# Strassen's seven products for a block's first matrix product, with the weight sums streamed from DRAM

## The chip, the cores and the metric

The kernel runs on one core of one Trainium2 chip, as one launch. The metric is the device time of the launch in microseconds (us), lower is better. A change of 0.5% (4.9 us) is about what a measurement of this kernel can tell from no change.

## The reference: what is computed

Causal attention with a decay, and then two feed-forward blocks, each a product up (512 to 2048), an elementwise function, and a product down (2048 to 512). The chain runs over 2304 tokens in float32:

```python
attn = softmax(q @ k.T / 8 + decay, causal); x = attn @ v      # 4 batches x 8 heads, 576 x 64 each
h = x @ w_in1                                                   # 2304x512 @ 512x2048
g = where(h >= 1, h, where(h <= -1, 0, (h + 1) ** 2 / 4))
x = g @ w_out1                                                  # 2304x2048 @ 2048x512
h = x @ w_in2                                                   # the product that is changed
P = a[0] + a[1] * h + a[2] * h**2 + a[3] * h**3
g = P / (1 + abs(b[0]) * abs(h) + abs(b[1]) * h**2 + 1e-6)
out = g @ w_out2
```

The weights come as 64-bit floats and are turned into 32-bit ones on the chip.

## The kernel before

Matmuls run on float32 operands of reduced width ("fp32r"). To keep the accuracy, each operand is split into a high part (a cast) and a low part (the rest), and each product is three matmuls: low by high, high by low, high by high. So for every tile ACT makes the high part and DVE or POOL the low one.

**Stages.** Attention (with early pieces of the first block as filler) takes the first 200 us or so. Then the first block runs to about 595 us and the second from there to the end. The tokens are cut into four chunks of 512 and one of 256 (`CH`, L698), the 2048 hidden columns into 16 groups `g` of 128. The second block takes one chunk after the other; for each of the 16 groups it does

- `gemm_in` (L728): 4 pieces of the contraction by 3 matmuls, each 128x128 weights by 128x512 tokens, into one PSUM bank `h`;
- `b_abs`, `b_sq`, `b_lin` (ACT, L769 to L776), `b_v` (POOL, L780), `b_t1`, `b_t2` (DVE, L784, L788), `b_ln`, `b_exp` (ACT, L791, L794), `b_t3`, `b_v3`, `b_t4` (DVE, L798, L801, L805): the rational function. After `b_t4` the bank `h` is free;
- `split_g_hi` (ACT, L745) and `split_g_lo` (POOL, L749);
- `gemm_out` (L820): four token pieces by 3 matmuls into four accumulators `a0` to `a3`, which stand in PSUM over all 16 groups.

There are four `h` banks (`HB`) and four accumulators: all eight banks of PSUM. At the end of a chunk the accumulators are copied out (`out_copy`) and stored.

**Weights.** Each 128x512 piece is loaded (`w_raw`), put together by one ACT and four DVE instructions (`w_steps`, L86), and, for those not needed yet, stored to DRAM (`w_store`) and loaded again later (`w_load`), cast and subtracted (`w_split`). That work for the second block lies in the first block's time, 42 such stores and loads in all. In the second block all its weights stand in SBUF.

**Order.** The program is written as tasks with a key, an engine or a choice of engines, an estimated duration, and the buffers that it takes and frees. `plan` (L273) places them one by one by the earliest start plus a small weight on the key, and the instructions are then written out in that order. Each engine runs its own list strictly in that order; what was estimated only decides the order. Loads and stores are all issued by SP, in order.

Of the kernel before, what the change touches and what calls it, by code (L numbers as in the profile page):

```python
# [7 lines left out]
F32 = mybir.dt.float32  # L8
# [10 lines left out]
def kernel(ctx, tc, qT, kT, v, f, w_in1, w_out1, w_in2, w_out2, a, b, out):  # L19
# [9 lines left out]
    P = 128  # L29
# [49 lines left out]
    wfd = dram.tile([2, NF, 2, P, DM], F32, name="wfd")  # L79

# [5 lines left out]
    def w_steps(m, g, half):  # L86
# [33 lines left out]
    def w_split(m, g, half):  # L120
        at = {}

        def s0():
            pool = wearly if g < W_EARLY else wpool["late"]
            at["s"] = wst.pop((m, g, half))
            at["w"] = [pool.tile([P, DM], F32R, tag=f"{x}{half}_{g}", name=f"w{x}{half}_{m}_{g}") for x in "hl"]
            ACT.copy(at["w"][0][:], at["s"])

        def s1(eng=POOL):
            hi, lo = at["w"]  # L130
            eng.tensor_tensor(out=lo[:], in0=at["s"], in1=hi[:].bitcast(F32), op=ALU.subtract)
# [116 lines left out]
    XR = 4  # L248
    XA = 3
# [3 lines left out]
    N_BUF = dict(S=SB, T=TB_, O=OB, P=PB, PT0=1, PT1=1, q=2, k=2, qs=2, ks=2, v=2, R=RB, x=1, cb=2, g=W_EARLY, c=2, s=SF, xa=XA, xr=XR, po=2, raw=2, d=2)  # L253
# [489 lines left out]
    def split_g_hi(g, n):  # L743
        gt[g] = [gp.tile([P, NM], F32R, tag=y, name=y)[:, 0:n] for y in ("gh", "gl")]
        ACT.copy(gt[g][0], mid[g][0])  # L745
# [74 lines left out]
    def gemm_out(m, x, g, d, first, last):  # L820
# [5 lines left out]
        for y, (gg, ww) in enumerate(((gl, wh), (gh, wl), (gh, wh))):  # L826
# [3 lines left out]
            else:  # L830
                PE.matmul(acc[x, d], gg[:, dd], ww[:], start=st, stop=sp)  # L831
# [17 lines left out]
    def out_copy(x, d, eng):  # L849
        os_[x, d] = stage.tile([P, DM], F32, tag="raw", name="osb", bufs=2)  # L850
        copy(eng, os_[x, d][:], acc.pop((x, d)))

    def out_store(x, d):
        t0 = C0[x % NCH] + d * P
        SP.dma_start(out[t0:t0 + P, :], os_.pop((x, d))[:])

# [89 lines left out]
    TN = 5, 5, 5  # L946
# [3 lines left out]
    CK, CL, W2S, W2L = 0.4, 10.0, 20.0, 3.0  # L950
# [3 lines left out]
    KXL = 1.0  # L954
    LOE = ['pool']
# [19 lines left out]
    passes = [(0, x, early) for x in range(FILL, HEAD)] + [(0, x, late) for x in range(HEAD)]  # L975
    passes += [(0, x, range(NF)) for x in range(HEAD, NCH)]
    passes += [(1, x, range(NF)) for x in range(NCH, 2 * NCH)]
# [14 lines left out]
    bufs.update({tag: [t_end] * k for tag, k in dict(h=HB, g=GB, t0=TN[0], t1=TN[1], t2=TN[2], raw=2, d=2, xr=XR, a0=1, a1=1, a2=1, a3=1).items()})  # L992
    bufs.update({f"x{k}": [] for k in range(KD)})


# [17 lines left out]
    prev_in = None  # L1013
    for p, (m, x, fs) in enumerate(passes):
# [3 lines left out]
        ca, cs, cd, cp = cost("act", n), cost("act", n, "ps"), cost("dve", n), cost("pool", n)  # L1018

        sx = [] if p else sx0  # L1020
        for kk in range(KD) if p else ():
            deps = [evac[x - NCH, kk]] if m == 1 else xstores(x, kk)
            t = xload = task(k0 - KXL, "sp", ld(n), lambda x=x, kk=kk: x_load(x, kk), deps + [xload], ("xr",))
            t = task(k0 - 0.5, "act", ca, lambda x=x, kk=kk: split_x_hi(x, kk), [t] + sx[:1], (f"x{kk}",))
            sx.append(task(k0 - 0.5, "dve", cd, lambda x=x, kk=kk: split_x_lo(x, kk), (t,), (), ("xr",)))
# [3 lines left out]
        if add:  # L1029
            for d in range(KD):  # L1030
                loads[d] = task(
                    k0 + 1, "sp", ld(n), lambda x=x, d=d: part_load(x, d), [lastpass[x, d]] + list(prev_evac), ("t2",)
                )
        outs = []
        for g in fs:
            key = base + sizes[p, g]
            one, end = g == fs[0], g == fs[-1]

            for kks in [(kk,) for kk in range(KD)] if one or end else [range(KD)]:
                deps = [prev_in, wd[m, g, 0]] + [sx[kk] for kk in kks if one]  # L1040
                prev_in = task(key, "pe", mm(n, 3 * len(kks)), lambda m=m, x=x, g=g, kks=kks: gemm_in(m, x, g, kks), deps,
                               ("h",) if kks[0] == 0 else (), tuple(f"x{kk}" for kk in kks) if end else ())
            t = tin = prev_in
# [17 lines left out]
            t = task(key, "act", ca, lambda g=g, n=n: split_g_hi(g, n), (t,), ("g",))  # L1061
            t = task(key, "pool", cp, lambda g=g: split_g_lo(g, POOL), (t,), (), ("t1",))

            for d in range(nd):
# [79 lines left out]
```

## Time and profile before

| | |
|---|---|
| median of 3 runs | 983.75 us (982.46 to 986.32) |
| profiled execution, first to last instruction | 984.3 us |
| PE (matmul) busy | 98% of the span |
| DVE, ACT, POOL busy | 74%, 64%, 46% |
| DMA | 125.15 MB, mean 127 GB/s |

The profiled execution has no time of its own beside its span; the span lies 0.55 us above the median of the runs. "Busy" is the time in which an engine had an instruction in it. Matmuls overlap: one of 128x512 is shown as some 0.39 us long, though the next starts 0.23 us later, so rates are read from starts. The profile names a group of instructions by line, engine and operation, with "output <- inputs".

### The profile page before, as it was taken

To read this page: it belongs to the slowest core of one execution; us is meant where nothing else is said; L and a number is where in the kernel's file an instruction comes from. 1 tells how busy PE (TensorE), PEld (TensorE's weight loads), DVE (VectorE), ACT (ScalarE), POOL (GpSimd) and SP (SyncE) were. 2 spreads that over 40 slices of the span, in tenths; PEclk is the share of its full clock that TensorE was granted. 3 is DMA by queue.
4 is the path that set the end of the run, shared out by engine and by line. 5 is a ranking of instruction groups with operands and counts; after the bars stand their busy time and mean duration, and the time that the engine had idled before them with its cause. 6 is when DMAs were issued, how large, how long until landed. Compare 5 with 4: busy or idle time off the path is not lost.

```text
span 984.3 us, 15503 instructions
## 1 busy us (share of the span) xinstructions
PE 964.6 (98%) x5124; PEld 784.3 (80%) x5124; DVE 729.0 (74%) x1379; ACT 629.6 (64%) x1324; POOL 457.0 (46%) x505
## 2 busy tenths in 40 slices
PE   8988999999999999999999999999999999999998
PEld 5656777777888788888888998888888888888887
DVE  7999888883876977877875679776667667666656
ACT  6988688884654433424333579776777667666666
POOL 4877746654655422222221225544444454444444
PEclk9999999999999999999999999999999999999999
DMA  6878589844563365665643651010101100010010
GB/s 224 260 258 251 174 272 293 263 162 166 194 232 118 96 226 155 188 205 161 221 151 123 177 172 33 1 44 1 43 1 44 43 1 22 0 43 1 1 44 22
DMA packets 66657, 125.15 MB, mean 127 GB/s; under 512 B 10048, under 2 KB 20944, under 8 KB 66576
## 3 DMA queue, kind: packets, MB, share of 16 engines
q1 hardware_dynamic: 66576, 124.16, 39.6%
q8 instruction: 40, 0.66, 0.3%
q14 instruction: 41, 0.34, 0.1%
HBM read 94.61 MB, written 29.51 MB: 126 GB/s over the span
## 4 chain that ended last, share of the span: by engine, by line
PE 85%; DVE 6%; DMA 3%; issue 2%; ACT 2%; SPq 1%; POOL 1%; DVEq 0%; POOLq 0%; ACTq 0%
PE h L735 38%; PE a L831 19%; PE a L829 17%; PE T L510 3%; PE O L547 2%; PE a L816 2%; PE S L446 2%; DVE P L486 1%; DVE xl L724 1%; DMA cb<-cd 1%; DMA R<-rcd 1%; PE S L437 1%; ACT P L498 1%; DVE wd L97 1%; DVE PT L360 0%
## 5 line engine op out<-in xcount | busy, mean ns | idle before, releaser
L749 POOL TENSOR_TENSOR gl<-t,gh 128x512 fp32r<-128x512 f32 (+1 forms) x160 | 195.4, 1222 | 292.1 <-ACT gh L745 224.8
L735 PE MATMUL h<-xl,wh 128*128 128x512 f32 (+1 forms) x640 | 236.7, 370 | 1.0 <-DVE xl L724 0.6
L735 PE MATMUL h<-xh,wl 128*128 128x512 f32 (+1 forms) x640 | 237.0, 370 | 0.0
L735 PE MATMUL h<-xh,wh 128*128 128x512 f32 (+1 forms) x640 | 235.7, 368 | 0.0
L745 ACT CAST gh<-t 128x512 fp32r<-128x512 f32 (+1 forms) x160 | 92.9, 581 | 124.0 <-PE a L831 47.9
L780 POOL TENSOR_TENSOR t<-t,t 128x512 f32<-128x512 f32 (+1 forms) x80 | 94.5, 1182 | 126.7 <-ACT t L773 121.1
L735 PEld LDWEIGHTS h<-xl,wh 128*128 128x128 f32 x640 | 120.8, 189 | 24.0 <-DVE xl L724 4.2
L735 PEld LDWEIGHTS h<-xh,wl 128*128 128x128 f32 x640 | 120.9, 189 | 20.4
L735 PEld LDWEIGHTS h<-xh,wh 128*128 128x128 f32 x640 | 120.8, 189 | 19.9
L831 PE MATMUL a<-wh,gl 128*128 128x512 f32 x288 | 112.3, 390 | 0.3 <-POOL gl L749 0.3
L831 PE MATMUL a<-wl,gh 128*128 128x512 f32 x288 | 112.2, 390 | 0.0
L831 PE MATMUL a<-wh,gh 128*128 128x512 f32 x288 | 112.1, 389 | 0.0
L829 PE MATMUL a<-gh,wl 128*128 128x512 f32 (+1 forms) x288 | 105.3, 366 | 0.0
L829 PE MATMUL a<-gl,wh 128*128 128x512 f32 (+1 forms) x288 | 105.3, 366 | 0.0
L829 PE MATMUL a<-gh,wh 128*128 128x512 f32 (+1 forms) x288 | 105.2, 365 | 0.0
L759 ACT ACTIVATE t<-t 128x512 f32<-128x512 f32 (+1 forms) x80 | 47.1, 589 | 83.5 <-DVE t L754 82.7
L798 DVE SCALAR_TENSOR_TENSOR t<-t,na,h 128x512 f32<-128x512 f32 (+1 forms) x80 | 55.4, 693 | 57.2 <-ACT h L794 56.1
L498 ACT ACTIVATE P<-P,nm 128x576 f32<-128x576 f32 (+2 forms) x144 | 83.6, 582 | 16.4 <-DVE nm L486 15.5
L754 DVE TENSOR_SCALAR t<-h 128x512 f32<-128x512 f32 (+1 forms) x80 | 50.6, 634 | 53.7 <-PE h L735 53.1
L784 DVE TENSOR_TENSOR t<-h,t 128x512 f32<-128x512 f32 (+1 forms) x80 | 51.0, 637 | 49.0 <-ACT t L776 48.6
L770 ACT ACTIVATE t<-h,ab 128x512 f32<-128x512 f32 (+1 forms) x80 | 51.8, 649 | 42.1 <-PE h L735 41.9
L238 POOL TENSOR_SCALAR_AFFINE_SELECT cb<-cb 128x128 f32<-128x128 f32 (+1 forms) x150 | 55.5, 381 | 43.7 <-DVE nm L486 33.9
(121 smaller groups left out, 1929.6 us busy)
## 6 DMA issues: line engine op xcount, KB each, us to landing
raw<-in_moe_w_in_dram SPq DMA_DIRECT2D x32, 512.0 KB
raw<-in_moe_w_out_dram SPq DMA_DIRECT2D x32, 512.0 KB
xr<-xd SPq DMA_DIRECT2D x48, 256.0 KB
wfd<-wd SPq DMA_DIRECT2D x42, 256.0 KB
wf<-wfd SPq DMA_DIRECT2D x42, 256.0 KB
cb<-cd SPq DMA_DIRECT2D x15, 576.0 KB
ks<-in_k_dram SPq DMA_DIRECT2D x16, 288.0 KB
qs<-in_q_dram SPq DMA_DIRECT2D x16, 288.0 KB
```

What stands on the lines that cost most here:

```text
L238: POOL.affine_select(out=t, in_=t, compare_op=ALU.is_ge, fill=-BIG, base=0, pattern=[[-1, n]], channel_multiplier=1,)
L498: ACT.activation(p, p, AF.Exp, scale=-1.0, bias=nm[pr][:, pos:pos + 1], accum_out=ls[pr][:, COL[pos]:COL[pos] + 1])
L735: PE.matmul(hps[g], ww[:, kk * P:(kk + 1) * P], xx[kk], start=(kk == 0 and y == 0), stop=(kk == KD - 1 and y == 2))
L745: ACT.copy(gt[g][0], mid[g][0])
L749: eng.tensor_tensor(out=lo, in0=mid.pop(g)[0], in1=hi.bitcast(F32), op=ALU.subtract)
L754: DVE.tensor_scalar(out=c, in0=hps[g], scalar1=-1.0, scalar2=1.0, op0=ALU.max, op1=ALU.min)
L770: ACT.activation(mid[g]["w"], hps[g], AF.Abs, scale=ab[:, 0:1])
L780: POOL.tensor_tensor(out=vv, in0=vv, in1=mid[g]["w"], op=ALU.add)
L784: DVE.tensor_tensor(out=t, in0=hps[g], in1=t, op=ALU.mult)
L798: DVE.scalar_tensor_tensor(out=t, in0=t, scalar=na[:, 0:1], in1=hps[g], op0=ALU.add, op1=ALU.mult)
L829: PE.matmul(acc[x, d], ww[:, dd], gg, start=st, stop=sp)
L831: PE.matmul(acc[x, d], gg[:, dd], ww[:], start=st, stop=sp)
```

## The change

For the four chunks of 512 tokens, `gemm_in` of the second block is done for two groups (2j, 2j+1) at a time by Strassen's method. The 512 contraction rows are halved, the two groups are the two halves of the output columns, and the 512 tokens are halved too. Seven products of half-size operands (`PRODUCTS`) take the place of eight: each is 2 pieces of the contraction by 3 matmuls of 128x128 by 128x256, so 42 narrow matmuls stand where 24 wide ones stood. Product 1 and 2 open the two `h` banks of the pair; products 6, 5 and 4 add onto what stands in a bank, after the value before was copied out to `sq` (`q_out`, on ACT or DVE: once after product 1, once after 6, and a wide one after 7). At the end `q_add` (DVE) adds the copies to each bank, and the elementwise function follows as before. The chunk of 256 is done as before.

The sums of the operands are made beforehand. For the weights: `q_sums` (POOL, eight 128x128 instructions a pair, in the first block's time), then high and low parts (`q_hi` on ACT, `q_lo` on POOL), stored to DRAM (`q_store`, eight stores of 256 KB a pair). For the tokens: `xq_sums`, `xe_hi`, `xe_lo` at each chunk's start. The weights of the second block's first product no longer stand in SBUF: for every pair and chunk they are loaded again by `q_load` (three loads of 512 KB and one of 256 KB a pair, two of 512 KB for the chunk of 256) into a ring of ten slots, which were the places of the first block's weights 6 to 15; slots 0 to 5 hold the token sums.

Further: three `d` buffers (`DB`) for two, four `t0` for five, `out_copy` takes a `d` buffer, `split_g_hi` may go to POOL in the second block, loads of partial sums are issued later (`PLG`), high and low weights share one tile, and the last pass of the first block is now chunk 3's groups 4 to 15 and no longer the chunk of 256.

```diff
+    wqd = dram.tile([NF // 2, 4, 2, P, DM], F32, name="wqd")
-    N_BUF = dict(S=SB, ..., po=2, raw=2, d=2)
+    N_BUF = dict(S=SB, ..., po=2, raw=2, d=DB)
...
+    def q_sums(j, i, e):
+        wg, wo = (wst[1, 2 * j + k, 0] for k in range(2))
+        a = [w[:, (2 * c + i) * P:(2 * c + i + 1) * P] for w in (wg, wo) for c in range(2)]
+        t = wsum[j, i] = t_new(j, "t0", DM, TN[0])
+        s1, s2, s3, s4 = (t[:, k * P:(k + 1) * P] for k in range(4))
+        eng = ENGINES[e]
+        eng.tensor_tensor(out=s1, in0=a[2], in1=a[3], op=ALU.add)
+        eng.tensor_tensor(out=s2, in0=s1, in1=a[0], op=ALU.subtract)
+        eng.tensor_tensor(out=s3, in0=a[0], in1=a[2], op=ALU.subtract)
+        eng.tensor_tensor(out=s4, in0=a[1], in1=s2, op=ALU.subtract)
...
+    def q_load(j, k, r, c0):
+        t = wring[j, k] = slot_tile(r, F32R, f"q{j}_{k}")
+        SP.dma_start(t[:, :, c0:].bitcast(F32), wqd[j, k, :, :, c0:].rearrange("y p n -> p y n"))
...
+    PRODUCTS = {
+        1: ((0, 0), (0, None, R), (1, L)), 2: ((0, HQ), (HQ, None, R), (0, R)), 6: (None, (None, 0, R), (1, L)),
+        3: (None, (HQ, None, L), (0, L)), 5: (None, (None, 0, L), (1, L)), 7: (None, (None, 1, L), (1, R)),
+        4: ((1, HQ), (None, 1, R), (1, R)),
+    }
+    def q_mul(x, j, n):
...
+        for i in range(HQ):
...
+            for y, (ww, xx) in enumerate(((wl, xh), (wh, xl), (wh, xh))):
+                PE.matmul(
+                    o, ww, xx, start=(i == 0 and y == 0 and n not in (6, 5, 4)),
+                    stop=(i == HQ - 1 and y == 2), skip_group_check=True,
+                )
+
+    def q_out(j, n, e):
+        h = hps[2 * j + 1]
...
+        if n == 7:
+            copy(e, sq[j][:, 0:3:2, :], h[:].rearrange("p (c n) -> p c n", n=QN))
+        else:
+            copy(e, sq[j][:, 1 if n == 1 else 3, :], h[:, L])
+
+    def q_add(j, gg):
+        h = hps[2 * j + gg][:]
...
+        DVE.tensor_tensor(out=h, in0=h, in1=s, op=ALU.add)
...
-    passes += [(0, x, range(NF)) for x in range(HEAD, NCH)]
+    passes += [(0, x, range(NF)) for x in range(HEAD, NCH)] + [(0, HEAD - 1, late)]
...
+                    p1 = mul(1, [prev_in, l0, sx[0], sx[1]], ("h",), fx("x0", "x1"))
+                    o1 = out_(1, p1, ("raw",))
+                    p2 = mul(2, [p1, sx[HQ], sx[HQ + 1]], ("h",), (f0,))
+                    p6 = mul(6, [p2, o1, l2, l3, sxe[0, 0], sxe[1, 0]])
+                    o6 = out_(6, p6)
+                    p3 = mul(3, [p6], (), fx("x2", "x3"))
+                    p5 = mul(5, [p3, o6], (), fx(*fe[0:2]))
+                    p7 = prev_in = mul(7, [p5, sxe[0, 1], sxe[1, 1]], (), (f2, f3))
+                    o7 = out_(7, p7)
+                    p4 = mul(4, [p7, o7, l1], (), (f1,) + fx(*fe[2:4]))
+                    for gg, pp in ((0, p3), (1, p4)):
+                        ready[g + gg] = task(
+                            key, "dve", cd, lambda j=j, gg=gg: q_add(j, gg), (pp, o1, o6, o7) + ((ready[g],) if gg else ()), (), ("raw",) if gg else ()
+                        )
```

What this does to the order, on PE in the second block's fourth chunk before: one group's first product ends and the product down of an earlier group follows (`h` is the first product's bank, `xh`, `xl` the tokens' parts, `wh`, `wl` the weights', `gh`, `gl` the parts of g).

```order
L735 MATMUL h_5_9629<-xh_3_9363,wl_1_5_6707 128x512
L735 MATMUL h_5_9629<-xl_3_9367,wh_1_5_6706 128x512
L735 MATMUL h_5_9629<-xh_3_9363,wh_1_5_6706 128x512
L831 MATMUL a_0_9014<-wh_1_14_7352,gl 128x512
L831 MATMUL a_0_9014<-wl_1_14_7353,gh 128x512
L831 MATMUL a_0_9014<-wh_1_14_7352,gh 128x512
L831 MATMUL a_1_9023<-wh_1_14_7352,gl 128x512
```

And on PE in the changed program's first chunk of the second block: the end of product 2, products 6, 3, 5 and 7, and a product down (`xe` are the token sums, `q` the slots of the ring).

```order
L967 MATMUL h_10_8035<-xh_3_7380,q_0_7742 128x256
L967 MATMUL h_11_8002<-xe_0_0_7080,q_2_7755 128x256 x3
L967 MATMUL h_11_8002<-xe_1_0_7225,q_3_7803 128x256 x3
L967 MATMUL h_10_8035<-xh_2_7379,q_2_7755 128x256
L967 MATMUL h_10_8035<-xl_2_7383,q_2_7755 128x256
L967 MATMUL h_10_8035<-xh_2_7379,q_2_7755 128x256
L967 MATMUL h_10_8035<-xh_3_7380,q_3_7803 128x256
L967 MATMUL h_10_8035<-xl_3_7384,q_3_7803 128x256
L967 MATMUL h_10_8035<-xh_3_7380,q_3_7803 128x256
L967 MATMUL h_11_8002<-xe_0_0_7080,q_2_7755 128x256 x3
L967 MATMUL h_11_8002<-xe_1_0_7225,q_3_7803 128x256 x3
L834 MATMUL a_1_7657<-w_1_6_7220,gl 128x512
```

Product 6 wrote bank h11; product 5 adds onto it again, and between them stand only the six matmuls of product 3, in which the copy of h11 has to be done. Over the 32 pairs, 23 of the 64 narrow copies have only six narrow matmuls beside them, 26 have these and three wide ones, and the rest more; the 32 wide copies have six wide matmuls or more.

On DVE in the second block before, one group's five instructions stand together, with one copy of an accumulator between:

```order
L784 TENSOR_TENSOR t_6_8970<-h_6_8944,t_6_8970 128x512
L788 SCALAR_TENSOR_TENSOR t_6_8970<-t_6_8970,na,h_6_8944 128x512
L798 SCALAR_TENSOR_TENSOR t_6_8970<-t_6_8970,na,h_6_8944 128x512
L801 SCALAR_TENSOR_TENSOR h_6_8944<-t_6_8971,h_6_8944 128x512
L360 COPY osb<-a_3_8331 128x512
L805 SCALAR_TENSOR_TENSOR t_6_8970<-h_6_8944,t_6_8970 128x512
L784 TENSOR_TENSOR t_7_9020<-h_7_8992,t_7_9020 128x512
```

In the changed program DVE has the additions (L984) and some of the copies (L363, `sq`) between them, and the groups are interleaved:

```order
L801 SCALAR_TENSOR_TENSOR t_6_7893<-t_6_7893,na,h_6_7787 128x512
L791 SCALAR_TENSOR_TENSOR t_7_7924<-t_7_7924,na,h_7_7761 128x512
L804 SCALAR_TENSOR_TENSOR h_6_7787<-t_6_7894,h_6_7787 128x512
L984 TENSOR_TENSOR h_8_7900<-h_8_7900,sq_7907 128x512
L808 SCALAR_TENSOR_TENSOR t_6_7893<-h_6_7787,t_6_7893 128x512
L801 SCALAR_TENSOR_TENSOR t_7_7924<-t_7_7924,na,h_7_7761 128x512
L984 TENSOR_TENSOR h_9_7879<-h_9_7879,sq_7907 128x512
L804 SCALAR_TENSOR_TENSOR h_7_7761<-t_7_7925,h_7_7761 128x512
L363 COPY sq_8016<-h_11_8002 128x256
L808 SCALAR_TENSOR_TENSOR t_7_7924<-h_7_7761,t_7_7924 128x512
L787 TENSOR_TENSOR t_8_7991<-h_8_7900,t_8_7991 128x512
L791 SCALAR_TENSOR_TENSOR t_8_7991<-t_8_7991,na,h_8_7900 128x512
```

Three pairs are now in DVE's hands at once: groups 6 and 7 end, 8 and 9 begin, and a copy for group 11 stands among them. In the second block's four wide chunks DVE gets 64 such additions, 40 narrow copies and 6 wide ones; ACT gets 24 narrow and 26 wide ones.

## Rows read from the trace of the kernel before

**Rows 1.** The page's head: span, busy time by engine, granted clock in 40 slices.

```profile
span 984.3 us, 15503 instructions
...
PE 964.6 (98%) x5124; PEld 784.3 (80%) x5124; DVE 729.0 (74%) x1379; ACT 629.6 (64%) x1324; POOL 457.0 (46%) x505
...
PEclk9999999999999999999999999999999999999999
```

**Rows 2.** Busy time by stretch: start:end length, each engine, clock, DMA share, GB/s.

```profile
300.00:350.00 50.00, 49.35 (x217) 40.20 (x216) 40.69 (x59) 22.76 (x40) 23.06 (x17) 1.00 0.37 116
450.00:500.00 50.00, 50.00 (x222) 41.42 (x221) 39.34 (x61) 19.57 (x32) 13.09 (x10) 1.00 0.67 209
608.10:696.20 88.10, 87.98 (x388) 72.49 (x387) 65.54 (x97) 65.14 (x109) 41.98 (x33) 1.00 0.06 19
696.20:783.70 87.50, 87.37 (x386) 72.03 (x385) 59.82 (x87) 61.89 (x103) 41.38 (x32) 1.00 0.08 25
783.70:871.20 87.50, 87.37 (x385) 72.02 (x385) 59.83 (x87) 61.90 (x103) 41.44 (x33) 1.00 0.06 19
```

**Rows 3.** Chain that ended last, 500 to 984 us: start, length, what.

```profile
696.24 2.72 PE h L735 x12
...
783.70 2.72 PE h L735 x12
...
871.16 2.72 PE h L735 x12
...
918.91 2.75 PE a L831 x12
921.66 2.87 PE h L735 x24
```

**Rows 4.** The same chain around PE's one wait for POOL near the end.

```profile
953.15 0.42 ACT gh L745
953.57 0.03 POOLq L749
...
954.04 0.04 issue
954.08 6.41 PE a L831 x27
```

**Rows 5.** Groups by form, 783.7 to 871.2 us: busy us, mean ns | idle before.

```profile
L798 DVE SCALAR_TENSOR_TENSOR t<-t,na,h 128x512 f32<-128x512 f32 x16 | 11.9, 746 | 14.0 <-ACT h L794 13.8
...
L801 DVE SCALAR_TENSOR_TENSOR h<-t,h 128x512 f32<-128x512 f32 x16 | 11.0, 688 | 0.0
...
L360 DVE COPY osb<-a 128x512 f32<-128x512 f32 x2 | 1.4, 688 | 0.2 <-PE a L831 0.2
```

**Rows 6.** Groups by form over the whole span: the half-width forms.

```profile
L735 PE MATMUL h<-xh,wh 128*128 128x256 f32 x128 | 36.2, 283 | 0.0
...
L780 POOL TENSOR_TENSOR t<-t,t 128x256 f32<-128x256 f32 x16 | 11.8, 739 | 6.5 <-ACT t L773 5.0 <-DVE t L798 1.4
...
L358 ACT COPY PT<-T 128x256 f32<-128x256 f32 x26 | 9.5, 365 | 1.1 <-PE T L510 1.1
...
L801 DVE SCALAR_TENSOR_TENSOR h<-t,h 128x256 f32<-128x256 f32 x16 | 6.7, 421 | 0.0
```

**Rows 7.** Busy time by stretch, in the chunk of 256 (columns as in Rows 2).

```profile
960.00:965.00 5.00, 5.00 (x37) 4.66 (x36) 4.74 (x13) 5.00 (x16) 3.57 (x5) 1.00 0.01 3
965.00:970.00 5.00, 5.00 (x38) 4.74 (x38) 4.52 (x13) 4.78 (x14) 2.66 (x5) 1.00 0.00 0
```

**Rows 8.** DVE in order of time in the first block: start, length.

```profile
400.87 0.68 DVE L113 SCALAR_TENSOR_TENSOR wd<-raw,wd 128x512 int32<-128x512 int32 x1
401.47 0.68 DVE L724 TENSOR_TENSOR xl<-xr,xh 128x512 fp32r<-128x512 f32 x1
402.28 1.30 DVE L97 TENSOR_SCALAR wd<-wd 128x512 f32<-128x512 f32 x1
```

**Rows 9.** POOL in order of time, same place.

```profile
401.75 1.54 POOL L749 TENSOR_TENSOR gl<-t,gh 128x512 fp32r<-128x512 f32 x1 [4.43 <-ACT gh L745]
```

**Rows 10.** Groups by form, 230 to 560 us, the first block.

```profile
L749 POOL TENSOR_TENSOR gl<-t,gh 128x512 fp32r<-128x512 f32 x56 | 77.5, 1386 | 167.2 <-ACT gh L745 165.2 <-issue 1.9
...
L107 DVE SCALAR_TENSOR_TENSOR wd<-raw,wd 128x512 int32<-128x512 int32 x46 | 38.4, 835 | 1.2
...
L131 DVE TENSOR_TENSOR wl<-wf,wh 128x512 fp32r<-128x512 f32 x12 | 8.8, 747 | 3.0 <-ACT wh L127 2.8
```

**Rows 11.** The page's GB/s in 40 slices of 24.6 us.

```profile
GB/s 224 260 258 251 174 272 293 263 162 166 194 232 118 96 226 155 188 205 161 221 151 123 177 172 33 1 44 1 43 1 44 43 1 22 0 43 1 1 44 22
```

More of the change, by code (lines that the diff above doesn't have):

```diff
@@ L248 @@
     XR = 4
+    DB = 3
     XA = 3
@@ L830, in gemm_out @@
             else:
-                PE.matmul(acc[x, d], gg[:, dd], ww[:], start=st, stop=sp)
+                PE.matmul(acc[x, d], gg[:, dd], ww, start=st, stop=sp)
     def part_load(x, d):
@@ new lines, in q_store, with xq_hi @@
+    def q_store(j, k):
+        hi, lo = wq.pop((j, k))
+        SP.dma_start(wqd[j, k, 0], hi[:].bitcast(F32))
+        SP.dma_start(wqd[j, k, 1], lo.bitcast(F32))
+    def q_load(j, k, r, c0):
+        t = wring[j, k] = slot_tile(r, F32R, f"q{j}_{k}")
+        SP.dma_start(t[:, :, c0:].bitcast(F32), wqd[j, k, :, :, c0:].rearrange("y p n -> p y n"))
+        if c0 == 0 and k < 2:
+            wt[1, 2 * j + k, 0] = (t[:, 0, :], t[:, 1, :])
+    def xq_hi(x, kk):
+        if kk == 0:
+            xsp[x] = [[xp.tile([P, NM], F32R, tag=f"x{y}{k}", name=f"x{y}{x}_{k}") for k in range(KD)] for y in "hl"]
+        c0 = 0 if kk >= HQ else QN
+        ACT.copy(xsp[x][0][kk][:, c0:], xraw[x, kk][:, c0:])
@@ L1013, with q_loads @@
     prev_in = None
+    ring = [0]
+    lastx = {}
+    def q_loads(j, ks, key):
+        at = {}
+        for k in ks:
+            r = RING[ring[0] % len(RING)]
+            ring[0] += 1
+            half = len(ks) > 2 and k == 1
+            at[k] = r, task(
+                key, "sp", ld(DM if half else 2 * DM), lambda j=j, k=k, r=r, c0=DM // 2 if half else 0: q_load(j, k, r, c0),
+                (qstored[j, k],), (took(r),)
+            )
+        return at
     for p, (m, x, fs) in enumerate(passes):
@@ L1018 @@
         ca, cs, cd, cp = cost("act", n), cost("act", n, "ps"), cost("dve", n), cost("pool", n)
+        quads = m == 1 and n == NM
         sx = [] if p else sx0
[L1021 to L1025, printed above, removed]
+        sxe = {}
@@ L1028 @@
         loads = {}
[L1029 to L1033, printed above, removed]
         outs = []
+        ready = {}
         for g in fs:
@@ L1037 @@
             one, end = g == fs[0], g == fs[-1]
[L1039 to L1043, printed above, removed]
+            j = g // 2
+            if add and g == fs[-PLG]:
+                for d in range(KD):
+                    loads[d] = task(
+                        key, "sp", ld(n), lambda x=x, d=d: part_load(x, d), [lastpass[x, d], prev_in, *prev_evac], ("t2",)
+                    )
```

230 lines of the change are left out of this document (198 added, 32 removed).

## The prediction

> **What bounds the kernel now.** The head of the profile's page comes first [rows 1]: PE is busy for 98% of the span, and the granted clock reads 9 in all 40 slices, which is the upper of its two levels, 2.4 GHz; there is no clock to win or lose before PE goes idle. The table by stretch comes next [rows 2]: in the second block's chunks PE is busy in 87.37 of 87.5 us, while DVE has 59.8, ACT 61.9 and POOL 41.4. So in the second block time goes only where PE's own instructions go. The chain of waits gives PE's rates [rows 3]: twelve matmuls of 128x512 take 2.72 us, 0.2267 each; 24 of 128x256, in the chunk of 256 tokens, take 2.87, 0.1196 each. A chunk of 512 is 16 groups of 24 wide matmuls, 16 x 5.44 = 87.04, and from one chunk's first matmul to the next (696.24, 783.70, 871.16) it is 87.46: 0.42 us of waiting a chunk. DVE waits most for ACT (14.0 us in front of L798) and not the other way [rows 5]. The kernel is bound by PE from end to end, and a matmul taken away is worth its slot as long as the other engines keep up.
>
> **The change part by part**
>
> Sums stand against the profiled span of 984.3 us, which lies 0.55 above the median of 983.75.
>
> 1. *The matmuls.* A pair of groups loses 24 wide ones, 24 x 0.2267 = 5.44 us, and gets 42 narrow ones, 42 x 0.1196 = 5.02 [rows 3]. That is 0.42 a pair and 32 pairs (four chunks by eight): **-13.4 us**. The saving is well under an eighth of 5.44 (0.68), since a narrow matmul costs 0.0063 more than half a wide one. These narrow rows have the same form as the new ones (128x128 weights, changed for every matmul, 256 columns), so I hold this for the surest term. At half price it would be 0.68 x 32 = 21.8, at this price it is 13.4; these are its ends.
> On the same point the Trainium skill ("TensorE: Matmul & The Clock Gate", section "Back-to-back issue gap") gives an isolated gap of N/2.4 ns plus 2.5. An estimate by it would be 24 x 0.2158 - 42 x 0.1092 = 0.59 a pair, 19.0 us in all. The trace disagrees: its 0.2267 at 512 columns stands 13 ns above 512/2.4, so the sum goes by the rows.
>
> 2. *The copies between products.* This is a wait that PE did not have: product 6 may not write its bank before the copy of product 1 is out, nor 5 before that of 6, nor 4 before the wide copy after 7. The narrow copy must fit between the last matmul of one product and the first of the next one on that bank. A 128x256 matmul is shown 0.283 long against a slot of 0.12 [rows 6], so its result is there some 0.16 after its slot; the rows around PE's wait for POOL show hand-overs of 0.03 and 0.04 [rows 4]; the copy is 0.421 by the half-width DVE row, 0.365 by the ACT one [rows 6]. Together 0.65 on DVE, 0.60 on ACT. Six narrow matmuls are 0.72. So with six beside it a copy just fits if its engine is free at that moment. DVE and ACT carry instructions of 0.6 us one behind another (DVE starts at 400.87 and 401.47 [rows 8]); an engine caught in one delays the copy by 0 to 0.6, less the 0.07 spare: 0 to 0.53, 0.23 in the mean if the arrival is random. By the order 23 of the 64 narrow copies have only this cover, 26 have 1.40 (three wide matmuls more), and the wide copies (0.688 [rows 5], 0.92 with hand-overs) have 1.36 or more. So only the 23 count: 0 at one end, 23 x 0.53 = 12.2 at the other, 23 x 0.23 = 5.3 for random arrival. The order puts the copies where DVE and ACT are near their end, and their queues wait for PE more often than the reverse; I take **+3.0**. Below nothing it cannot be: a copy gives PE nothing.
>
> 3. *DVE's load.* In a chunk it gets 16 additions of 0.688, about 10 narrow copies of 0.421, one or two wide ones, and some 2.5 us more work on the tokens: 59.8 + 11.0 + 4.2 + 1.0 + 2.5 = 78.5 us, in a chunk that is now 8 x (5.02 + 5.44) = 83.7 of PE. That is 94%. In the chunk of 256 DVE already works 4.74 and 4.52 of 5 us while PE shows 5.00 [rows 7], so it can be done; cost 0 in the forecast, and the nearness is a rival below. ACT goes from 61.9 to about 68.
>
> 4. *The start of a chunk.* Each of the four wide chunks has eight half-width sums and four more casts and subtractions in front of it (a half-width one on POOL is 0.739 [rows 6]). Before, a chunk's start cost 0.42 [rows 3]. I take twice that, **+1.7** over four chunks; the ends are 0 (all is made under the chunk before) and 8 (2 us each, one POOL sum and its cast late).
>
> 5. *The entry into the second block.* The first chunk's window was 88.1 against 87.5 [rows 2]. By the order its first additions of work on DVE stand only a few instructions ahead of the products that need their banks free. **+1.0**, ends 0 and 5.
>
> 6. *The first block's extra work.* POOL gets 64 subtractions or additions of 128x128 (0.37 to 0.739 each: at most the half-width row, at least half of it; 24 to 47 us), and 32 subtractions of 128x512 at 1.386, 44 us [rows 10]. In the stretches read POOL is busy for 23 and 13 of 50 us [rows 2], so some 350 us of that block have room for 91. ACT gets 16 casts, about 10 us, and is busy there for 20 to 23 of 50. DVE loses 16 subtractions at 0.747 [rows 10], 12 us. But a POOL instruction lengthens DVE's: L97 took 1.30 us from 402.28 while POOL's subtraction ran from 401.75 for 1.54 [rows 8, 9], and L107 is 0.835 in the mean where an undisturbed one of that size shows 0.68 [rows 10, 8]. At worst the doubled POOL time adds the same 0.155 again to some 200 DVE instructions, 32 us, less the 12. DVE stands idle for 10 us in each 50 [rows 2], about 70 in this stretch: it fits. The Trainium skill ("SBUF — State Buffer", section "SBUF: two separate sides") calls the port pair of these two engines an exclusive lock held for a whole instruction; the 1.30 agrees. Cost **0**, ends 0 and +14 (the 32 us fall where PE waits for DVE, less half hidden).
>
> 7. *The loads.* A pair now takes 1.835 MB from DRAM in about 10.5 us, 175 GB/s, where the second block moved next to nothing; slices of the page reach 293 [rows 11]. The ring holds two and a half pairs, so a load can be some 20 us ahead of its use. **0**. SP has nothing else to do there but the tokens and the output. The high parts that may go to POOL have no row of their kind; POOL has half its time free in a chunk (41.4 of 87.5), so I bound them by its full subtraction (1.386) and by nothing, off PE's path in both cases.
>
> Sum: -13.4 + 3.0 + 1.7 + 1.0 = -7.7; 984.3 - 7.7 = 976.6, and on the basis of the median **976.0 us**.
>
> **Rivals**
>
> - *More of the gain arrives.* The copies find their engines free and boundaries cost what they did: -13.4 alone, or with narrow matmuls at half price -21.8. For it: DVE's and ACT's idle time in the block; against the half price: 0.1196 in the rows. About 970.5, at the half price 962 and, with the waits of the sum, 968.
> - *DVE becomes the bound.* It needs 78.5 us a chunk, and its in-order queue also waits for ACT's logarithm and exponential (14.0 us of idle in front of L798 [rows 5]). If it can be kept busy for 90% at most, a chunk is 78.5/0.90 = 87.2 us, the length before: nothing of the gain is left in the block but the first microseconds, about 982. Against it: the 95% of [rows 7].
> - *The copies stop PE (slower).* A copy, as any instruction, waits behind what stands ahead of it in its engine's queue; on DVE that is often an instruction which itself waits for ACT or for an addition that waits for another product. If PE stops for more than (13.4 - 2.7)/32 = 0.33 us a pair, the change costs more than it gives. At 0.8 a pair it is 984.3 - 13.4 + 2.7 + 25.6 = 999; with both narrow copies of a pair at the 0.53 above, 34 us, 1007. For it: DVE and ACT at 94 and 81%, and 23 copies without slack; against it: 41 of 64 have twice the cover, and a wait of one copy gives the queues time to catch up.
> - *The first block is overloaded (slower).* Step 6 at its upper end: +14, about 990.
>
> **How the numbers follow.** A change of less than 0.5% (4.9 us) can't be told from none, which puts the bounds at 978.8 and 988.7. The forecast (972.5 to 978.8) has 0.44, more of the gain 0.20, DVE as the bound 0.17, PE stopped by copies 0.14, the first block 0.05. So faster 0.64, the same 0.17, slower 0.19. The range for 8 in 10 reaches from 968 (half price with waits) to 990 (the first block's end); left out are most of the copies' case and the full 962. The likeliest case's own range is 972.5 to 978.8.
>
> **What would show it.** Step 1: successive first products of chunks 84 to 85 us apart, six narrow matmuls in 0.72. Step 2: PE's idle time with the copies as releaser adds up to about 3 us; 25 or more is the slower rival. Step 3: DVE busy for about 93% of a wide chunk with PE above 98%; PE idle behind DVE's additions or L808 would make DVE the bound. Steps 4 and 5: PE's gaps at chunk starts under 1 us, at the entry near 1. Step 6: the first block's last product down near 595 us as before. Step 7: no wait of PE on a load of the ring. Narrow matmuls at another price than 0.1196, or a block that ends later with PE idle, would make the prediction wrong.

## The result and the profile after

The changed kernel takes 995.35 us (median of 4, 995.0 to 999.02) beside 983.53 for the kernel before on the same chip: ratio 1.0125, 95% interval 1.0103 to 1.0146. It is slower by 1.2%; the forecast was 976.0 with a range to 990.

The page's head, answering to [rows 1]:

```profile
span 993.7 us, 17463 instructions
...
PE 961.0 (97%) x5700; PEld 801.0 (81%) x5700; DVE 806.5 (81%) x1484; ACT 653.1 (66%) x1392; POOL 593.0 (60%) x652
...
PEclk9999999999999999999999999999999999999999
```

POOL has 136 us more work, DVE 78. PE's busy time fell by 3.6 us only, because a matmul is shown longer than its slot, so a short stop between two matmuls still reads as busy. The exact measure is PE's **loss**: the time from each matmul's start to the next one's, less its slot (0.2267 us at 512 columns, 0.1196 at 256, [rows 3]), added up over a stretch. All losses below are worked out so from the matmul starts of the traces.

| PE's loss, us | 240 to 300 | 300 to 344 | 344 to second block | second block to end |
|---|---|---|---|---|
| before | 0.6 | 1.3 | 0.2 | 2.2 |
| after | 7.0 | 0.6 | 11.0 | 12.0 |

The second block is counted from its first product: 581.06 us before, 590.16 after. With the 13.4 us won by the slots this makes -13.4 + 6.4 - 0.7 + 10.8 + 9.8 = +12.9 us, beside 11.8 between the medians. (The two profiled spans differ by 9.4 only: the one of before has a granted clock of 0.96 and 0.97 in the two stretches from 50 to 150 us of attention, the one of after 1.00 in both, and attention's last product starts 3.6 us earlier there.)

By stretch (columns as in [rows 2]), first of before, then of after:

```profile
240.00:300.00 60.00, 60.00 (x264) 48.88 (x263) 45.19 (x62) 35.41 (x63) 38.70 (x28) 1.00 0.60 203
...
500.00:550.00 50.00, 50.00 (x264) 43.14 (x263) 32.59 (x54) 17.98 (x34) 10.50 (x10) 1.00 0.40 125
...
592.00:920.00 328.00, 327.62 (x1454) 270.75 (x1453) 232.55 (x339) 239.47 (x403) 159.09 (x124) 1.00 0.07 21
```

```profile
240.00:300.00 60.00, 56.68 (x235) 44.61 (x235) 48.95 (x62) 33.33 (x58) 33.38 (x26) 0.97 0.51 171
...
500.00:550.00 50.00, 44.92 (x289) 40.34 (x288) 44.65 (x60) 24.04 (x51) 36.15 (x40) 0.98 0.73 250
...
592.00:920.00 328.00, 322.39 (x2023) 289.01 (x2023) 280.00 (x444) 249.50 (x439) 202.82 (x165) 1.00 0.60 200
```

In the first block DVE is at 44.65 of 50 us in the worst stretch, POOL at 36.15 where it had 10.50, and PE has 5 us of open idle time. In the second block PE is short of 5.6 us of 328. Who ended PE's waits is best read from the weight loads (PEld), which show a stop before the matmul behind them does. From 240 to 300 us (columns: who waited for whom, us in total, times, longest):

```profile
PEld h L738 <- DVE xl L727: 4.4, 6, 1.0
PEld h L738 <- ACT xh L723: 1.8, 1, 1.8
```

From 344 to 590 us:

```profile
PEld a L832 <- ACT t L361: 3.6, 1, 3.6
PEld h L738 <- DVE xl L727: 3.1, 5, 1.1
PEld a L832 <- POOL gl L752: 1.6, 2, 1.0
PEld a L832 <- DVE t L845: 1.0, 2, 0.6
```

and in the second block, 592 to 925 us:

```profile
PEld h L967 <- DVE sq L363: 4.9, 7, 1.7
PEld h L967 <- ACT sq L361: 3.0, 5, 0.9
PEld a L834 <- DVE t L845: 1.9, 1, 1.9
PEld h L967 <- ACT t L776: 0.9, 1, 0.9
```

No wait for a load of the ring is among them. The longest wait, 3.38 us from 544.08 us on, stands under ACT, but ACT waits for DVE (ACT's and DVE's rows in order of time):

```profile
546.74 0.63 ACT L762 ACTIVATE t<-t 128x512 f32<-128x512 f32 x1 [6.74 <-DVE t L757]
547.28 0.35 ACT L361 COPY t<-a 128x256 f32<-128x256 f32 x1
```

```profile
545.01 1.09 DVE L114 SCALAR_TENSOR_TENSOR wd<-raw,wd 128x512 int32<-128x512 int32 x1
546.03 1.87 DVE L757 TENSOR_SCALAR t<-h 128x512 f32<-128x512 f32 x3
```

From 538.33 to 546.03 us DVE has only five conversion steps and one subtraction of a weight's low part, 7.7 us in all. Its first step of the elementwise function, L757, comes behind them; ACT stands 6.74 us for it, and the copy of the accumulator that PE needs (L361) comes behind that in ACT's queue.

A small part of the first block's loss is the clock. Around this longest wait the table by stretch has

```profile
547.00:549.00 2.00, 1.32 (x3) 1.12 (x4) 2.00 (x4) 2.00 (x5) 0.00 (x0) 0.66 1.05 393
549.00:551.00 2.00, 2.00 (x6) 1.52 (x6) 1.10 (x3) 1.77 (x5) 1.74 (x2) 0.50 1.00 293
551.00:553.00 2.00, 2.00 (x11) 1.64 (x10) 2.00 (x3) 1.22 (x3) 1.12 (x2) 0.99 0.94 352
```

0.50 is the lower level, 1.2 GHz. The trace has such a fall here and another at 257.5 us, behind four waits of 0.7 to 1.6 us. By the longer slots there each costs some 1.7 us, together 3.4 of the 18.5 that are lost from 240 us to the second block. Before has none from 104 us to its last matmul.

In the second block the chain of waits shows the products' price, answering to [rows 3] (start, length, what):

```profile
893.98 2.93 PE h L967 x24
...
901.32 3.43 PE a L834 x15
904.75 2.93 PE h L967 x24
```

24 narrow matmuls in 2.93 us or less, 15 wide ones in 3.43; the first products of the second, third and fourth chunk start at 668.21, 752.27 and 839.02 us: 84.1 and 86.8 us a chunk where it was 87.46. (The 86.8 is the order: 12 wide matmuls more lie between these two starts than between the two before. PE's loss is some 3.0 us in either.)

### The profile page after: what moved, and what is told of

Read it like the earlier page. It is cut to its first block, busy times and chain, and to the rows that moved or that the text cites. A ratio compares the mean times of both kernels' runs of the same rounds, so it can differ in the third digit from the quotient of the medians.

```text
span 993.7 us, 17463 instructions
## 1 busy us (share of the span) xinstructions
PE 961.0 (97%) x5700; PEld 801.0 (81%) x5700; DVE 806.5 (81%) x1484; ACT 653.1 (66%) x1392; POOL 593.0 (60%) x652
## 4 chain that ended last, share of the span: by engine, by line
PE 58%; DVE 18%; DMA 6%; ACT 6%; POOL 6%; issue 5%; SPq 1%; DVEq 0%; POOLq 0%; ACTq 0%
PE a L834 16%; PE h L738 12%; PE h L967 12%; PE a L832 8%; PE T L513 3%; DVE wd L108 3%; DVE wd L114 2%; PE O L550 2%; PE S L449 2%; PE a L819 2%; DVE wd L98 2%; DVE wd L102 1%; DVE xl L727 1%; DMA wfd<-wd 1%; POOL gl L752 1%
## 5 line engine op out<-in xcount | busy, mean ns | idle before, releaser
L738 PE MATMUL h<-xh,w 128*128 128x512 f32 (+1 forms) x640 | 196.6, 373 | 1.6 <-ACT xh L723 1.4
L834 PE MATMUL a<-w,gh 128*128 128x512 f32 x576 | 178.8, 392 | 0.0
L832 PE MATMUL a<-gh,w 128*128 128x512 f32 (+1 forms) x576 | 162.7, 368 | 0.0
L738 PEld LDWEIGHTS h<-xh,w 128*128 128x128 f32 x640 | 117.8, 190 | 22.4 <-ACT xh L723 1.8
L361 ACT CAST gh<-t 128x512 fp32r<-128x512 f32 (+1 forms) x146 | 84.0, 576 | 71.4 <-DVE t L766 28.0
L834 PEld LDWEIGHTS a<-w,gh 128*128 128x128 f32 x576 | 108.8, 189 | 18.7
L738 PE MATMUL h<-xl,w 128*128 128x512 f32 (+1 forms) x320 | 119.9, 375 | 3.5 <-DVE xl L727 3.4
L832 PEld LDWEIGHTS a<-gh,w 128*128 128x128 f32 x576 | 104.9, 190 | 17.5
L834 PE MATMUL a<-w,gl 128*128 128x512 f32 x288 | 113.5, 394 | 1.5 <-DVE t L845 1.5
L967 PE MATMUL h<-xe,q 128*128 128x256 f32 x768 | 109.8, 285 | 4.1 <-DVE sq L363 2.5
L832 PE MATMUL a<-gl,w 128*128 128x512 f32 (+1 forms) x288 | 107.0, 371 | 4.8 <-ACT t L361 3.2
L757 DVE TENSOR_SCALAR t<-h 128x512 f32<-128x512 f32 (+1 forms) x80 | 50.1, 631 | 42.3 <-PE h L738 42.1
```

What stands on the lines that cost most here:

```text
L361: ACT.copy(out, src)
L738: PE.matmul(hps[g], ww[:, kk * P:(kk + 1) * P], xx[kk], start=(kk == 0 and y == 0), stop=(kk == KD - 1 and y == 2))
L757: DVE.tensor_scalar(out=c, in0=hps[g], scalar1=-1.0, scalar2=1.0, op0=ALU.max, op1=ALU.min)
L832: PE.matmul(acc[x, d], ww[:, dd], gg, start=st, stop=sp)
L834: PE.matmul(acc[x, d], gg[:, dd], ww, start=st, stop=sp)
L967: PE.matmul(o, ww, xx, start=(i == 0 and y == 0 and n not in (6, 5, 4)), stop=(i == HQ - 1 and y == 2), skip_group_check=True,)
```

## The experiments

Two things had to be told apart: what happened in the first block, 17 us, and in the second, 10. All runs are the changed kernel with the edits shown. e1, f1, g1, b1 and k1 leave out or replace a part of the arithmetic, so their output is not the one asked for; the other runs compute all of it. Runs of before beside them had medians of 983.4 to 984.3.

**POOL's new work taken out** (e1), the order of every engine kept:

```diff
-        eng.tensor_tensor(out=s1, in0=a[2], in1=a[3], op=ALU.add)   # and s2, s3, s4
+        ENGINES[e].memset(t, 0.0)
...
-        ENGINES[e].tensor_tensor(out=lo, in0=src, in1=hi[:].bitcast(F32), op=ALU.subtract)
+        wq[j, k] = (hi, hi[:])
```

> Same order on every engine. Left out: the 64 weight sums (a memset of the sums' tile stands in for each four) and the 32 subtractions of the low parts (the high part is stored twice); casts, stores and loads stay. POOL loses some 75 us of work in the first block from 344 us on. Theory A (POOL's new work lengthens DVE's instructions and DVE makes PE late): the 10 to 12 us that PE loses between 344 and 590 us go, L108 falls from 1.10 us towards 0.85, and the time falls from 995.4 to 984 to 987. Theory B (the chunk of 256 now stands among the conversions): the loss between 470 and 550 us stays, time 992 to 995. In both the 6 us lost between 246 and 275 us stay, since no such work has begun there.

Measured: 985.4 us, 10 less than the changed kernel. PE's loss from 344 us to the second block fell from 11.0 to 0.3, that of 240 to 300 stayed at 7.0, that of the second block at 11.9. So the sums' preparation costs 10 us, and none of it through ACT's casts or the stores, which were kept. Theory B (the pass order) is out.

**The pass order of before** (e2):

```diff
-    passes = ... [(0, x, late) for x in range(HEAD - 1)]
-    passes += [(0, x, range(NF)) for x in range(HEAD, NCH)] + [(0, HEAD - 1, late)]
+    passes = ... [(0, x, late) for x in range(HEAD)]
+    passes += [(0, x, range(NF)) for x in range(HEAD, NCH)]
```

> The first block's passes in the order of before: chunk 3's late groups in their old place, the chunk of 256 last. Theory B: the 9 us that PE loses between 470 and 550 us go, and some of them come back at the entry into the second block, where the token sums' places are free later: 988 to 992. Theory A: POOL's work is the same and stands over the same DVE work, so the loss only moves: 994 to 998.

Measured: 999.38 us. The loss from 344 to 590 is 10.7, as before the edit, and the entry into the second block loses 5.5 (590 to 640 us) where it lost 2.2. B falls here too; the new pass order helps.

**Two `d` buffers** (e3) and **the third one late** (f2):

```diff
-    DB = 3
+    DB = 2                                        # e3
...
+    bufs["d"] = [t_end, t_end, t_end + 70.0]      # f2, with DB = 3
```

> Two d buffers for three. Theory C (the third buffer lets conversions start earlier and stand in DVE's queue ahead of the tokens' low parts): the 6 us lost between 246 and 275 us go, time near 989. Rival: the loss there is DVE's lengthened instructions or another effect of the new order, and stays; and with two buffers a conversion waits longer for POOL's subtraction, so the later stretch loses more: 996 to 1005.

> The planner gets the third d buffer only 70 us later by its own clock, so that the conversions at 240 to 300 us stand as with two, and the prepared sums still have three. Theory C: PE's 7 us of loss between 240 and 300 us fall to about 0.5 as with two buffers, and the rest stays near the change's: 988 to 990. Rival: the order that follows is another one and loses elsewhere what is won: 993 to 997.

Measured: 1001.41 and 987.28 us. Both bring the loss of 240 to 300 us from 7.0 to 0.5 and 0.4. With two buffers the last weight sum starts at 582 us and not at 532, and the entry into the second block loses 19.6 us in its first 50 (from 579.8 us on), where the changed kernel loses 2.2; with the third one late the rest stays (8.5 from 344 us on). So the third buffer itself costs 6.5 us at the place where it first comes free, and is needed later. DVE's rows at that place, in the changed kernel:

```profile
243.76 0.81 DVE L98 TENSOR_SCALAR wd<-wd 128x512 f32<-128x512 f32 x1 [1.29 <-ACT wd L94]
244.60 1.40 DVE L102 TENSOR_SCALAR wd<-wd 128x512 int32<-128x512 int32 x1
245.93 1.78 DVE L727 TENSOR_TENSOR xl<-xr,xh 128x512 fp32r<-128x512 f32 x1
247.63 1.77 DVE L108 SCALAR_TENSOR_TENSOR wd<-raw,wd 128x512 int32<-128x512 int32 x1
```

and in the run with the third buffer late:

```profile
243.91 0.69 DVE L728 TENSOR_TENSOR xl<-xr,xh 128x512 fp32r<-128x512 f32 x1 [1.72 <-ACT xh L724]
244.52 1.52 DVE L98 TENSOR_SCALAR wd<-wd 128x512 f32<-128x512 f32 x1
246.07 1.40 DVE L102 TENSOR_SCALAR wd<-wd 128x512 int32<-128x512 int32 x1
```

With a buffer to spare a conversion stands ahead of the tokens' low part `xl` in DVE's queue and not behind it, and PE waits for `xl` at that place.

**Why POOL's work costs DVE and PE time.** Three explanations were left: POOL's and DVE's instructions keep each other out (A1); POOL frees the `d` buffers late and ACT's queue stands behind the next conversion (A2: in the changed kernel ACT's L94 waits 11.3 us for POOL); POOL's queue is just late with `gl` (A3). f1 keeps POOL's work and takes the hold on `d` away (the sums, and the low parts whose operand stands in `d`, read a weight tile that stands in SBUF all the time); g1 keeps POOL as busy and takes its reads away:

```diff
-        wg, wo = (wst[1, 2 * j + k, 0] for k in range(2))                # f1
+        wg, wo = (wt[0, 15, k][0].bitcast(F32) for k in range(2))
...
+        for _ in range(4):                                                # g1, for four sums;
+            ENGINES[e].memset(t, 0.0)                                     # three for a low part
```

> Same order. POOL's 64 sums and the first 16 of each 32 subtractions' operands are read from a weight tile that stands in SBUF all the time, so the sums come out of other weights; POOL's work keeps its count, sizes and place, but no longer holds the d buffers that the next conversion needs. Theory A1 (the shared port: POOL's work lengthens DVE's instructions): L108 and L114 stay at about 1.03 us after 344 us and PE's loss between 400 and 590 us stays near 10.5: 993 to 996. Theory A2 (POOL frees the d buffers late, ACT's queue stands behind the next L94, and PE behind ACT): ACT's 11 us of waiting for POOL at L94 go, and with them 5 to 10 us of PE's loss: 985 to 990.

> Same order. In place of the sums and subtractions POOL writes zeros: four memsets of 128x512 for four sums, three for a subtraction, at 0.53 us each by the run without them, so that POOL is about as busy as in the changed kernel and at the same places, but reads nothing from SBUF; the sums and low parts are left out. Theory A1 (what counts is that POOL's reads and DVE's keep each other out): DVE's L108, L98 and L102 fall back to 0.71, 0.66 and 0.47 us, PE's loss between 400 and 590 us falls from 10.5 to 0 to 2, time 985 to 987. Theory A3 (POOL's queue is late: gl and the d buffers come late because POOL is busy): the loss stays at 8 or more, 993 to 996, with DVE's instructions short. If DVE's instructions stay long, any instruction of POOL does it, not its reads alone, and the time stays as well.

Measured: 995.17 us (f1) and 987.19 (g1). In f1 ACT's L94 no longer waits for POOL at all, and the loss from 344 us on only goes from 11.0 to 9.1: A2 is worth at most 1.8 us. In g1 it goes to 1.5 although POOL is busy for longer, by the rows of 344 to 580 us, first of the changed kernel, then of g1:

```profile
344.00:580.00 236.00, 229.93 (x1176) 195.40 (x1175) 187.07 (x263) 102.86 (x191) 144.62 (x149) 0.99 0.66 223
```

```profile
344.00:580.00 236.00, 235.45 (x1218) 202.05 (x1217) 177.82 (x272) 107.89 (x200) 154.30 (x216) 1.00 0.68 230
```

So A3 is out and A1 stands, with one reservation. g1 changed two things more: POOL's sums no longer wait for DVE's conversions (9.9 us in the changed kernel), and a memset is shorter (some 0.57 us each) than a subtraction (1.4 to 1.5). f1 has the first of these too and keeps 9.1 us of loss; the second no run separates from the reads. DVE's conversion steps show A1, 344 to 580 us by form (busy us, mean ns | idle before), in the changed kernel, in e1 without POOL's work, and in g1:

```profile
L114 DVE SCALAR_TENSOR_TENSOR wd<-raw,wd 128x512 int32<-128x512 int32 x31 | 32.0, 1033 | 0.8
L108 DVE SCALAR_TENSOR_TENSOR wd<-raw,wd 128x512 int32<-128x512 int32 x30 | 30.8, 1028 | 0.6
L98 DVE TENSOR_SCALAR wd<-wd 128x512 f32<-128x512 f32 x30 | 23.0, 766 | 10.0 <-ACT wd L94 9.9
L102 DVE TENSOR_SCALAR wd<-wd 128x512 int32<-128x512 int32 x30 | 20.6, 688 | 0.6
```

```profile
L114 DVE SCALAR_TENSOR_TENSOR wd<-raw,wd 128x512 int32<-128x512 int32 x31 | 28.1, 906 | 0.8
...
L108 DVE SCALAR_TENSOR_TENSOR wd<-raw,wd 128x512 int32<-128x512 int32 x31 | 21.9, 706 | 0.7
L98 DVE TENSOR_SCALAR wd<-wd 128x512 f32<-128x512 f32 x30 | 19.8, 660 | 6.5 <-ACT wd L94 6.3
L102 DVE TENSOR_SCALAR wd<-wd 128x512 int32<-128x512 int32 x30 | 14.2, 474 | 0.6
```

```profile
L114 DVE SCALAR_TENSOR_TENSOR wd<-raw,wd 128x512 int32<-128x512 int32 x31 | 27.6, 889 | 0.8
L108 DVE SCALAR_TENSOR_TENSOR wd<-raw,wd 128x512 int32<-128x512 int32 x31 | 24.9, 805 | 0.7
...
L102 DVE TENSOR_SCALAR wd<-wd 128x512 int32<-128x512 int32 x31 | 22.1, 712 | 0.6
L98 DVE TENSOR_SCALAR wd<-wd 128x512 f32<-128x512 f32 x30 | 19.6, 653 | 5.9 <-ACT wd L94 5.8
```

In f1, where POOL reads as much as in the changed kernel, L114 has 1088 ns, L108 1038 and L102 797. L114 and L108 read two tensors from SBUF: beside e1, L114 is longer only where POOL's new work reads, and L108 by 322 ns there and by 99 against memsets. L102 reads one and is as long against writes alone; L98 reads one too and is not longer against them. DVE is busy for 187.1 us of 236 in the changed kernel, 172.0 without POOL's work and 177.8 against memsets; in these three, which have the same order, PE's loss goes with it: 11.0, 0.3 and 1.5 us.
The Trainium skill ("SBUF — State Buffer", section "SBUF: two separate sides") says that a DVE instruction with two SBUF inputs is locked out only by a POOL instruction that reads SBUF, one in a two-port mode by any. L114's 1033, 889 and 906 ns (changed kernel, g1, e1) agree, L108's 1028, 805 and 706 for the greater part. L102's 688, 712 and 474 fit an instruction in a two-port mode and L98's 766, 653 and 660 do not; in which mode either runs, no run here shows.

**The low parts on DVE** (f2d), and the sums too if the planner likes (f2c), both with the third buffer late:

```diff
-    QE = ['pool']
+    QE = ['dve', 'pool']     # f2c: sums and low parts; f2d: low parts on ['dve'] alone
```

> As the run with the third d buffer late, and the sums and their low parts may go to DVE or POOL, as the planner finds earlier. A subtraction is 0.7 us on DVE and 1.4 on POOL. A1: fewer POOL instructions lie over DVE's, DVE does some 10 to 25 us more itself; PE's loss of 10 us between 400 and 590 falls to 5: 983 to 986. A2: the d buffers come free sooner: 981 to 985. Rival (DVE is the scarce engine in the first block): no change against the run before it or worse, 989 to 995.

> As the run with the third d buffer late; the 32 subtractions of the low parts all on DVE, the sums on POOL. POOL loses 45 us and DVE gets some 24. A2: the buffers come free within a DVE instruction and ACT's wait for POOL at L94 goes: 982 to 986. A1: a POOL subtraction lengthened DVE's work by up to its own length, so 24 us for at most 31: 985 to 989. DVE as the scarce engine: 989 to 995.

Measured: f2d 981.49 us (ratio to before 0.9973, 0.9958 to 0.9989), f2c 997.94. In f2d DVE does 26 us of subtractions more than in f2 and is busy for 189.9 us of 236 where f2 has 186.4, with L102 at 471 ns; the loss from 344 us on is 3.3 for 8.5. So DVE's busy time is not the measure: it rises and PE loses less. The planner also made another order for f2d, and how much of the gain is the order is not shown. f2c is a miss of all theories: POOL is even less busy (79 us of the 246 from 344 to 590) and the loss is 21.0. Its chain of waits shows sums and low parts on DVE one behind another ahead of the first block's own steps, with a store of 5.23 us among them; PE waits 13.4 us for DVE's `t` (L767), and behind these stops the granted clock falls to 1.2 GHz twice. Taking work from POOL is no gain if what takes its place stands in front of PE's supplier in DVE's queue.

**Both causes out** (k1: e1's edit and the third buffer late):

```diff
+        ENGINES[e].memset(t, 0.0)                     # for the four sums
+        wq[j, k] = (hi, hi[:])                        # no low part
+    bufs["d"] = [t_end, t_end, t_end + 70.0]
```

> Both causes taken away: POOL's sums and subtractions left out as in the first run (a memset for four sums, the high part stored twice), and the third d buffer late. If these two make up the whole loss of the first block, PE loses 0.5 to 2 us between 240 us and the second block, and the time is 995.4 - 10 - 6.5, 978 to 980.5. If the two overlap, 981 to 986.

Measured: 980.23 us, 3.2 below before (ratio 0.9975, 0.9961 to 0.9988). The first block's loss from 240 us on is 2.0, about that of before, so this run isolates the second block: -13.4 + 11.8 - 2.2 = -3.8 by the slots and losses, -3.2 measured.

**The copies between products** (b1), and all of them on ACT (i2, on top of f2d):

```diff
-            copy(e, sq[j][:, 1 if n == 1 else 3, :], h[:, L])
+            copy(e, sq[j][:, 1 if n == 1 else 3, 0:2], h[:, 0:2])     # b1; wide ones likewise
...
+        s = wt[1, 0, 1][0].bitcast(F32)                             # what q_add adds
...
-    QOE = ['act', 'dve']
+    QOE = ['act']                                                       # i2
```

> Same order. In the second block the copies between products move 2 columns (4 for the wide ones), and the additions read a weight tile in place of the copies, so the result is left out there. If the copies' own length and lateness make PE wait in front of products 6, 5 and 4, the 9.5 us of PE's waits in the second block fall to 2 to 4: 987 to 990. If PE waits for engines that are late as a whole (DVE at 85%), 4 or less goes: 991 to 994.

> The run with the low parts on DVE and the third d buffer late, and all copies between products on ACT. If PE's waits in front of products 6, 5 and 4 come from DVE being in the midst of another instruction, they fall from 8 us by 2 to 4 and the time from 981.5 to 978 to 980. If ACT (81% busy, and in the logarithm's and exponential's chain) is as likely to be late, no change or worse: 981 to 986.

Measured: b1 990.93 us, 4.4 less, between the two expectations; the second block's loss falls from 12.0 to 8.1. The additions wait for no copy there either, so 3.9 us is the most that the copies' length can be worth. PE's waits for copies halve, by the weight loads' waits in b1 (592 to 925 us):

```profile
PEld h L967 <- DVE sq L363: 2.6, 4, 1.5
PEld a L834 <- DVE t L845: 1.9, 1, 1.9
PEld h L967 <- ACT sq L361: 1.7, 4, 0.5
```

A copy of 2 columns takes 0.156 us for 0.421 and still PE waits 4.3 us for it, so about half of the copies' waits is not their length; what stands ahead of them in their engine's queue is the likely rest, which no run takes away by itself. i2: 980.57 us (ratio 0.9970, 0.9957 to 0.9983); the weight loads' waits for copies go from 7.9 us (f2d) to 4.1, 1.2 at PE's own products are new, and the second block's loss goes from 11.9 to 10.3. The loss from 344 us on rises from 3.3 to 4.9, and the time is not told apart from f2d's. It is the fastest complete version here, 0.3% under before, less than the 0.5% that the prediction called no change.

**Two buffers, low parts on DVE, a sixth `t2`** (i1):

```diff
-    DB = 3
+    DB = 2
-    TN = 4, 5, 5
+    TN = 4, 5, 6
...
+    QLE = ['dve']
```

> A version meant to win, result complete: low parts on DVE, two d buffers as before the change, and the 2 KB spent on a sixth t2 buffer. If the d buffers come free soon enough with DVE's shorter subtraction, the loss in the first block is 0 to 3 us, time 979 to 982. If two buffers hold up the conversions as in the run with two alone, the sums come late and the entry into the second block loses 5 to 15 us: 987 to 998.

Measured: 985.54 us, a miss: 6.1 us of loss from 344 us on (5.9 of it in 500 to 550) and 4.4 in 590 to 640.

## Why the prediction was wrong

- *Step 6 failed: the first block's work at 0.* It cost 10.8 us, inside the ends of 0 and 14, but that takes most of step 1. The first block's last product down, its sign, starts at 608.3 us and not at 590.7. The lengthening of DVE was sized well (32 us at the worst; the 184 conversion steps between 230 us and the second block took 27.1 us more in all, and DVE was busy for 23.9 us more after the moved subtractions). What failed is "it fits". Idle time averaged over 50 us says nothing of a queue: DVE's instructions are in order, and a conversion step stretched to 1.0 us or more stands ahead of `xl`, of the `t` that ACT waits for, or of a partial sum, and PE waits behind these (3.1, 3.6 and 1.0 us by the weight loads). The loss stands where DVE is fullest (7.7 of the 11.0 us in 500 to 550, DVE 44.65 of 50 us). The rival for this, at 990 and with 0.05, was the right one. Nor did I price that a stop of PE can be followed by a stretch at the lower clock.
- *No step priced the third `d` buffer*, one of the edits: 6.5 us by e3 and f2, since it moved conversions ahead of `xl`. With step 6 that is 17 us in the first block, beyond the upper end of all that I had there.
- *Step 1 held for the narrow matmuls and missed the wide ones.* 24 narrow ones take 2.88 to 2.93 us, and outside stops their mean slot in the second block is 0.1192; the half price is out. But the wide ones, taken as unchanged, have 0.2300 there where before had 0.2270: 887 of them, 2.9 us. What lengthens them is not shown; the loads' traffic alone does not, since from 344 to 590 us, at 222 GB/s, they take 0.2270.
- *Step 2 was low.* Waits with a copy as releaser are 4.9 + 3.0 = 7.9 us by the weight loads; taking the copies' length away gives back 3.9. I had 3.0 and ends of 0 and 12.2. (PE's own rows show only 3.6, since a matmul is shown longer than its slot.) Only some dozen products waited at all, so the narrow covers mostly held.
- *Steps 4 and 5*, forecast at 1.7 and 1.0, measured 2.8 in two waits: 1.9 at the entry (610.4 us, DVE's L845, the last partial sums of the first block), and 0.9 at the start of the fourth chunk (ACT's L776). All of the second block is 9.8 against 5.7 forecast: 7.7 in stops, 2.1 in slots.
- *One reading was wrong without harm to the sum.* 696.24, 783.70 and 871.16 us are not the chunks' first matmuls, which start at 653.45, 740.95 and 828.41; the distance is the same. But the stretch from 608.10 that step 5 took for the entry lies 27 us behind the block's first product, and in the 50 us behind that product the kernel before loses only 0.1.
- *Step 3 and the rival DVE as the bound.* In the two middle chunks DVE is busy for 74.7 of 84.1 and 74.9 of 86.8 us, 89 and 86%, less than the 94% worked out per full chunk, and PE's losses are single waits, not DVE's rate. The 94% added up row lengths, which overlap: in the later of these chunks DVE's rows add up to 83.6 us. *Step 7 held*: 200 GB/s, no wait on a load.
- The slower rival that I gave most (copies, 999) was near in time and wrong in place: most of the time went in the first block.

## What to carry to other kernels

Price work that is made "beforehand" where it is made: on an engine whose instructions lengthen those of the engine that feeds PE it costs more than its own time, and average idle time of an in-order queue is no cover. When a change adds POOL instructions over DVE's, multiply the lengthening that the trace already shows and look at what stands behind the lengthened instruction. An extra buffer is a change of order: it lets work with a far deadline stand ahead of work with a near one.

## What the runs showed of the hardware

Moving 32 subtractions from POOL (1.36 and 1.51 us each) to DVE (0.87 and 0.85), f2 against f2d (which has another order too), raised DVE's busy time by 3.4 us of 236 only, since L102 went from 715 to 471 ns and L98 from 769 to 533: DVE paid nearly as much for POOL doing them. Memsets on POOL (128x512, 0.56 to 0.58 us in the mean in g1) lengthen L102 as the subtractions do, and neither L98 nor L114.

After PE's stops in the first block the granted clock fell from 2.4 to 1.2 GHz, once behind a single stop of 3.38 us and once behind four of 0.7 to 1.6 us; the single ones of 1.62 us at 610 and 1.48 us at 674 us in the second block were followed by none. The stops alone do not decide it: f1 has the same four stops at 246 to 256 us and no fall behind them, and a single stop of 2.62 us is followed by a fall in i2 (538 us) and by none in f2d (537 us). The stretch from 240 to 300 us loses 6.1 us in f1 and 7.0 with the fall, so the fall there costs 0.9 in the end, less than its longer slots.
